# Scores and mask of a head in one 128-row contraction, and a first pair handled in two halves

## The chip, the cores and the metric

The kernel runs on one core of a Trainium2 chip. The metric is the device time of one execution in microseconds; lower is better. The core has five engines with an instruction queue each: TensorE (PE; its weight loads are shown as PEld), VectorE (DVE), ScalarE (ACT), GpSimd (POOL) and SyncE (SP), which mostly issues DMA transfers. Every engine works its queue strictly in order and waits on semaphores for the others.

## The reference

Attention over selected chunks, followed by a gated linear unit with a causal convolution. Batch 4, 8 heads, 768 tokens, head size 64, chunks of 32 tokens, float32 in and out.

```python
k_min, k_max = min and max of k over each chunk of 32 tokens
ub = np.sum(np.maximum(q[:, :, :, None, :] * k_min[:, :, None, :, :],
                       q[:, :, :, None, :] * k_max[:, :, None, :, :]), axis=-1)
ub = np.where(pos[:, None] // chunk >= np.arange(nc)[None, :], ub, -1e9)
top_chunks = np.argsort(ub, axis=-1)[..., -6:]
mask = (chunk of key j is in top_chunks) & (pos[:, None] >= pos[None, :])
attn = softmax(where(mask, q @ k.T / sqrt(64), -1e9));  attn_out = attn @ v

x = attn_out with its heads side by side                       # (4, 768, 512)
gate = sigmoid(sum_k conv_w[k] * xp[:, k:k+S, :])              # 5 taps, causal
out = (gate * (x @ w_val)) @ w_out
```

Query tokens below 192 have at most six chunks to choose from, so no chunk is masked for them.

## The kernel before

**Pairs.** Two heads are handled together as a pair; there are 16, four to a batch. The head size is 64, so the two heads of a pair fill the 128 partitions: head 0 in rows 0 to 63, head 1 in rows 64 to 127 (`HP`).

**Stages of a pair.** K and Q are loaded token by token and turned by TensorE (`tr`, line 472). ScalarE evicts K to the 16-bit `Kh` (`kev`, 478) and Q, times 64, to `Qh` (`qev`, 514). VectorE takes minimum and maximum of every chunk of K from PSUM (`kred`, 484), GpSimd makes the small factors `KB` from them (`ksmall`, 504 to 509). For the bound, Q is split into a 16-bit high part and a rest (`ql`, 522 or 537) and into their positive parts `rh` and `rl` (556, 560, 565). TensorE multiplies these with `KB` (`ub`, 590; for the first four pairs `ubd`, 605). VectorE finds the top six by an eight-largest instruction (`top`, 615 or 644) and writes 1 for each chunk that is not selected to `NS` (`cmp`, 653).

**Mask.** `NS` has the query tokens on partitions and has to be turned to have chunks there. Pairs 0 to 8 do this on TensorE (`selT`, 663) with a copy to `MT` (`mcopy`, 675 on ScalarE for pairs 0 to 2, 677 on VectorE for 3 to 8). Pairs 9 to 15 (`SELD`) do it with a transposing DMA from SyncE's queue (`mdma`, 665).

**Scores.** Scores of a head are computed with the keys on partitions, in six PSUM groups (`BANKS`) of 512, 512, 512, 512, 384 and 256 query columns. A head contracts over 64 rows, so two heads run side by side on the two halves of the array (line 692). For columns from token 192 on, a second matmul per head adds a penalty (line 697): `E` holds -51200 where a key belongs to a chunk, contracted over 64 rows with `MT`. ScalarE takes the exp to `P` (706), GpSimd clears the diagonal blocks (`tri`, 714).

**After the scores.** TensorE multiplies `P` with V and a column of ones (`av`, 735), VectorE divides (743, 744), the result is turned by TensorE (760, 762) or, for pairs 8 to 14, by DMA (`xd`, 765). It goes out to DRAM (`xw`, 778) and back in another layout (`xs`, 782, tile `XS`) for the convolution, which uses 64x32 pieces of the array (793). Then come tanh (799), the value product per batch (816), the gate (824), the output product (840), its eviction (850, 847) and the store (855).

**The order.** Nothing is ordered at run time. Each operation is entered into a graph with an engine, an assumed duration, what it reads and writes, and a key: `p * PERIOD + OFF[stage] + DELTA[stage][p]`. A list scheduler in the program works through the graph and gives each engine the ready operation with the smallest key; it also hands out the eight PSUM banks. The result is one fixed list per engine. `MODE_SWITCH` is the scheduler's price for a change between whole-array and divided-array matmuls. `lock` marks VectorE operations during which it starts no GpSimd work. In the first 26 us, `fill` puts dummy matmuls into TensorE's planned gaps.

Of the kernel before, what the change touches and what calls it, by code (L numbers as in the profile page):

```python
# [11 lines left out]
FP = mybir.dt.float32  # L12
# [7 lines left out]
CH = 32  # L20
# [16 lines left out]
SELD = range(9, NPAIR)  # L37
HP = (slice(0, 64), slice(64, 128))
MP = (slice(0, NCH), slice(64, 64 + NCH))
SM = 192  # L40
# [10 lines left out]
SCORE = [0.40, 0.435, 0.442, 0.445, 0.35, 0.325]  # L51
# [3 lines left out]
for _bi, _segs in enumerate(BANKS):  # L55
    for _col, _jt, _q0, _n in _segs:
        for _i in range(_n // 128):
# [3 lines left out]
            MT=2, on=2, xT=8, XS=3, g=8, gv=8, osb=4, scr=4)  # L61

PERIOD = 13.2487
OFF = dict(wdg=689.463, wbig=-821.57, cw=-638.386, load=-26.611, ktr=-313.189, qtr=-239.905, kev=166.913,
           qev=-383.955, ksm=148.208, spl=244.528, vc=540.922, ub=-278.308, top=-291.823, selT=-172.354,
           sc=-256.234, ex=-198.66, av=-117.315, nrm=263.685, tox=-134.594, xs=14.333, conv=-269.157,
           tanh=-393.525, val=323.303, gv=522.471, out=327.173, ev=91.258)
# [3 lines left out]

EARLY = (0, 1, 2)
QLA = (1, 2, 3)
# [5 lines left out]
    wdg=(-0.259, 11.176, 5.417, 0.077, -1.668, 4.13, 5.35, 1.029, 15.805, 3.045, -3.731, 0, -3.953, 0, 0, 0),  # L79
    wbig=(4.521, -1.173, -4.251, -0.71, -6.836, -7.879, -1.406, -13.108, -0.554, -12.202, 1.098, -1.574,  # L80
        -2.473, -1.919, 10.286, 15.067),
    cw=(0, 0, 1.049, 0, -3.776, -0.311, -0.92, -4.993, -0.92, -6.529, -7.915, -11.168, 0.948, 0, -8.06, 3.706),
    load=(-9.433, -20.842, -32.131, -6.001, -15.044, -1.827, -12.02, 13.514, 5.014, 13.589, 14.754, 5.081,
        -6.414, 4.609, -2.48, -7.659),
    ktr=(-2.8, -5.035, -2.262, 2.581, 0.902, 9.564, 0, 0, 10.923, 1.13, -0.491, -0.903, 0, 13.091, 0, -1.519),
    qtr=(0, -0.071, 9.102, 0, 3.757, 12.574, 5.717, -4.881, -3.114, -14.91, -6.366, 2.222, 0.471, 9.573, 4.53,
        0),
    kev=(-2.229, -2.16, 2.677, -4.88, -7.568, -10.347, 4.307, -2.668, 4.622, 3.276, -0.858, 6.192, 2.689,
        -4.962, -5.387, -2.214),
    qev=(-4.798, -6.316, 0, 0.959, 0, -3.801, -4.226, -3.069, -0.528, -1.223, 0, 0, -6.763, 0, 2.363, 0.065),  # L90
    ksm=(13.028, 3.364, 1.499, 0.759, -1.548, -11.855, -3.051, 6.295, -16.352, 0.972, -0.612, 7.732, 0, -1.146,
        0, -2.064),
    spl=(1.262, 11.137, -16.05, -1.69, -4.33, -6.699, -40.483, 4.206, 3.281, 19.318, -19.036, -16.32, 12.261,
        -5.656, 10.037, 0.718),
    vc=(1.748, -27.085, -4.307, 0, -5.756, -0.371, -4.158, 0.266, 21.35, -3.576, 0, 0.35, 5.25, -0.034, 12.327,
        7.302),
    ub=(-1.261, -1.704, -7.813, 3.091, -4.015, -14.948, 0, 2.233, 2.322, 0, -7.876, 13.15, -8.595, -0.126,
        -18.872, -17.052),
    top=(5.067, 2.169, 6.094, 9.602, 14.045, 13.01, -0.156, -5.897, 1.098, 0.084, 2.913, 2.943, 2.121, -0.002,
        0, 11.724),  # L100
    selT=(10.026, 2.182, -0.498, 4.774, -0.189, -0.821, 5.123, 1.014, 0.873, 3.056, 12.093, 5.215, 1.134,
        -0.467, -2.246, 0.26),
    sc=(-3.684, 2.323, 6.111, 6.751, -2.871, -17.678, -30.23, -1.526, -13.134, -1.219, 1.476, -1.084, 0.465,
        26.912, 1.856, -0.962),
    ex=(0.518, -1.916, 26.612, -0.555, 1.908, 0, -0.304, 1.658, -12.071, 1.68, 0, -4.112, -1.281, 0, -6.681,
        3.816),
    av=(8.141, 23.715, 0, -3.234, 0.925, 0.036, -16.039, -1.518, -0.512, -1.918, -1.793, -11.122, 7.414, 0,
        4.536, 0.431),
    nrm=(0.219, -0.69, -2.27, -15.358, -3.955, -5.17, 1.725, 5.097, 2.136, 76.904, 10.773, 11.399, 0.327,
        10.314, 6.848, 16.568),  # L110
    tox=(5.083, -9.624, -3.531, 16.222, -3.29, 7.771, 0.127, 7.218, -3.237, 2.083, -3.821, -1.177, 0.557,
        -9.325, 3.562, 1.286),
    xs=(-0.589, -20.407, -3.618, 3.816, 0, -1.25, 2.952, -7.384, 2.493, 1.773, 2.46, -0.962, -12.556, 1.62,
        -0.613, 2.66),
    conv=(-0.411, -7.384, -5.199, -0.916, -1.613, -3.484, 2.127, -5.739, 0, 0, 3.767, 12.228, 5.66, -7.854,
        6.314, 3.519),
    tanh=(-0.597, 0.252, -0.042, 6.877, 0, 0, 20.177, 16.64, 2.504, 0.308, 20.302, -0.547, 4.277, 0.743, 5.404,
        6.23),
    val=(0.746, 0, 0, -4.309, -5.054, 0.632, 3.993, -168.145, 0, 0, 4.124, 1.076, -6.197, -6.958, -8.508,
        -6.597),  # L120
    gv=(5.505, -3.972, 0, 7.879, 16.599, -0.597, 3.312, -14.616, -0.18, 0, 4.163, 0.738, 0.401, -3.09, -5.366,
        4.144),
    out=(-0.646, 3.026, -0.113, -7.77, -3.659, 3.789, 4.916, -4.962, 2.461, 0, -1.067, 11.205, -13.796, -2.374,
        -0.072, 0.251),
    ev=(9.081, -6.619, 0.125, -22.323, 0, 0, -4.231, -5.332, 22.655, 3.336, 2.632, -2.286, -26.622, -11.207,
        4.364, 10.267),
# [8 lines left out]
class Graph:  # L135


    def __init__(self, nbuf):
        self.nbuf, self.ops = nbuf, []
        self.reads, self.writes, self.wars, self.after = {}, {}, [], []  # L140

    def op(self, name, eng, occ, key, emit, r=(), w=(), war=(), ps=(), lat=None, mode=None, after=(), dma=None, tail=None,
           lock=False):
        o = Op()
        o.dma, o.tail, o.lock = dma, DMA_TAIL if tail is None else tail, lock
# [15 lines left out]
    def link(self):  # L161
# [3 lines left out]
        def back(x):  # L165
            n = self.nbuf.get(x[0])
            if n is None or len(x) < 2:
                return ()
            y = (x[0], x[1] - n) + x[2:]
            return self.reads.get(y, []) + self.writes.get(y, [])  # L170
# [118 lines left out]
MODE_SWITCH = 0.04  # L289
# [23 lines left out]
def graph(off, period, nbuf):  # L313
# [3 lines left out]
    def key(stage, p, x=0.0):  # L317
        return p * period + off[stage] + off.get((stage, p), 0.0) + x
# [29 lines left out]
    def c_hm():  # L348
        for hh in range(2):
            t.nc.vector.memset(t.hm[HP[hh], hh, :], QS)  # L350
            t.nc.vector.memset(t.hm[HP[hh], 1 - hh, :], 0.0)
# [28 lines left out]
    def c_e():  # L380
        t.nc.scalar.activation(out=t.E.rearrange("p (c t) -> p c t", t=CH),
                               in_=t.id32[:, 0:NCH].unsqueeze(2).to_broadcast([128, NCH, CH]), func=AF.Copy, scale=PEN)
    G.op("E", "ACT", 0.75, -100, c_e, r=[("id32",)], w=[("E",)])
# [31 lines left out]
    last.append(G.op("wout", "POOL", 2.0, key("wbig", 4), w_out, w=[("wout",)], dma=3.2))  # L415
# [4 lines left out]
    cwr = G.op("cwrep", "DVE", 0.7, key("cw", 0), w_rep, r=[("cw",)], w=[("cw4",)])  # L420
# [27 lines left out]
    for p in range(NPAIR):  # L448
# [14 lines left out]
        for x, name in enumerate(("kn", "qn", "vn")):  # L463
            G.op(f"{name}{p}", "SP", 0.6 if x == 2 else 1.1, key("load", p, x + (3 if x == 2 else 0)), load(name), w=[(name, p)], dma=2.0)
# [408 lines left out]
    for o in later:  # L873
        o.deps.add(byname["ksm1"])
# [156 lines left out]
```

## Time and profile before

| | us |
|---|---|
| median of three runs | 188.27 (188.14 to 188.57) |
| the profiled execution, whole | 191.16 |
| its span in the trace | 189.5 |
| first score matmul / last one starts | 14.87 / 155.55 |
| first exp starts | 16.46 |

In the trace, a row of the timeline gives start, length, engine, line, operation, output and inputs, shape and count. A matmul's length runs from its start to a modelled end, and matmuls overlap; what one costs is read from the distance between starts. Groups that the prediction does not show:

```profile
L706 ACT ACTIVATE P<-b 128x512 f16<-128x512 f32 (+2 forms) x192 | 88.8, 593 | 6.2 <-PE b L697 2.1
L484 DVE TENSOR_REDUCE km<-b 128x12 f32<-128x384 f32 x64 | 32.5, 549 | 6.1 <-PE b L472 3.6
L478 ACT ACTIVATE Kh<-b 128x384 f16<-128x384 f32 x32 | 15.9, 529 | 3.7 <-PE b L472 2.9
L514 ACT ACTIVATE Qh<-b 128x384 f16<-128x384 f32 x32 | 15.2, 508 | 3.4 <-PE b L472 3.3
...
XS<-scr SPq DMA_DIRECT2D x32, 194.0 KB, 4.2
...
MT<-NS SPq DMA_TRANSPOSE x7, 4.2
xT<-on SPq DMA_TRANSPOSE x7, 4.9
```

The first four rows are groups of instructions: line, engine, operation, shapes and count, then their busy time in us and the mean of one in ns, then the engine's idle time just before them and what ended it. The last three are DMA issues with the median time from issue to landing. ScalarE's instructions overlap their neighbours by some 0.15 us, so twelve exps of 5376 columns take 5.34 us in the timeline where their means add up to more.

### The profile page before, as it was taken

How to read it: one execution, taken by the hardware profiler on the slowest of the kernel's cores; microseconds unless marked ns; L12 is line 12 of the kernel's file. 1: busy time of each engine (PE TensorE's matmuls, PEld its weight loads, DVE VectorE, ACT ScalarE, POOL GpSimd, SP SyncE). 2: the span in 40 equal slices, each digit the busy share in tenths (PEclk: the TensorE clock that was granted, in tenths of full speed). 3: DMA queues.
4: the chain of work that ended last, by engine and by line, in shares of the span. 5: the costliest groups of instructions: out<-in, count | busy, mean ns of one | idle time of the engine just before them, and what ended most of it. 6: DMA issues, size and time to landing. Idle time of an engine off the chain costs nothing.

```text
span 189.5 us, 7611 instructions
## 1 busy us (share of the span) xinstructions
PE 177.9 (94%) x2994; PEld 118.3 (62%) x2994; DVE 138.0 (73%) x452; ACT 145.3 (77%) x326; POOL 88.1 (46%) x187
## 2 busy tenths in 40 slices
PE   7879999999999999999999999999999897799992
PEld 2566768777677658667766765767666554444540
DVE  4696998699989987999996889897964321621551
ACT  4659999989979788799949998969999496056221
POOL 5336899997981851716154563538464021000000
PEclk9999999999999999999999999999999999999999
DMA  6999979998899988877999999999969969967335
GB/s 143 220 218 210 212 172 196 225 214 195 218 232 263 219 201 205 192 179 211 168 221 215 218 201 205 179 221 196 193 173 196 251 194 194 321 219 244 121 120 212
DMA packets 97105, 38.77 MB, mean 205 GB/s; under 512 B 86810, under 2 KB 91950, under 8 KB 97070
## 3 DMA queue, kind: packets, MB, share of 16 engines
q1 hardware_dynamic: 95966, 37.25, 91.0%
q0 software_dynamic: 1104, 1.05, 3.8%
q8 instruction: 23, 0.38, 0.9%
q14 instruction: 12, 0.10, 0.1%
HBM read 27.34 MB, written 9.47 MB: 194 GB/s over the span
## 4 chain that ended last, share of the span: by engine, by line
PE 68%; DMA 9%; ACT 7%; DVE 5%; POOL 5%; issue 2%; SPq 2%; ACTq 0%; DVEq 0%; POOLq 0%
PE b L735 10%; PE b L692 9%; PE b L840 9%; PE b L816 9%; PE b L472 9%; PE b L793 8%; DMA XS<-scr 7%; PE b L697 6%; PE b L590 5%; ACT P L706 4%; DMA qn<-in_q_dram 2%; DVE km L484 1%; PE b L663 1%; ACT Qh L514 1%; PE b L760 1%
## 5 line engine op out<-in xcount | busy, mean ns | idle before, releaser
L706 ACT ACTIVATE P<-b 128x512 f16<-128x512 f32 (+2 forms) x192 | 88.8, 593 | 6.2 <-PE b L697 2.1
L714 POOL TENSOR_SCALAR_AFFINE_SELECT P<-P 128x512 f16<-128x512 f16 (+1 forms) x64 | 33.9, 551 | 44.9 <-ACT P L706 44.8
L692 PE MATMUL b<-Qh,Kh 64*128 64x128 f16 (+3 forms) x384 | 39.8, 259 | 0.6 <-ACT P L706 0.6
L484 DVE TENSOR_REDUCE km<-b 128x12 f32<-128x384 f32 x64 | 32.5, 549 | 6.1 <-PE b L472 3.6
L697 PE MATMUL b<-MT,E 64*128 64x128 f16 (+4 forms) x352 | 36.9, 255 | 0.1
L824 DVE SCALAR_TENSOR_TENSOR gv<-g,b 128x384 f16<-128x384 f32 x32 | 17.1, 549 | 15.6 <-PE b L816 13.9
L735 PE MATMUL b<-VA,P 128*128 128x65 f16 x672 | 27.7, 194 | 0.0
L735 PEld LDWEIGHTS <-P 128*128 128x128 f16 x672 | 24.4, 98 | 4.3 <-issue 2.3
L692 PEld LDWEIGHTS <-Kh 64*128 64x128 f16 x384 | 17.6, 94 | 12.8 <-issue 8.0
L799 ACT ACTIVATE g<-b 128x384 f32<-128x384 f32 x32 | 14.1, 497 | 14.4 <-PE b L793 14.3
L816 PE MATMUL b<-xT,wval 128*128 128x384 f16 x128 | 24.5, 327 | 0.0
L840 PE MATMUL b<-wout,gv 128*128 128x512 f16 x96 | 23.0, 379 | 0.0
L850 ACT ACTIVATE osb<-b 128x512 f32<-128x512 f32 x21 | 12.9, 637 | 10.6 <-PE b L840 6.7
L697 PEld LDWEIGHTS <-E 64*128 64x128 f16 x352 | 17.3, 94 | 4.7 <-issue 2.0
L793 PE MATMUL b<-XS,WD 64*32 64x384 f16 x640 | 16.5, 324 | 3.3 <-DMA XS<-scr 3.3
L478 ACT ACTIVATE Kh<-b 128x384 f16<-128x384 f32 x32 | 15.9, 529 | 3.7 <-PE b L472 2.9
L744 DVE TENSOR_TENSOR on<-b,rcp 128x384 f16<-128x384 f32 x32 | 17.8, 558 | 1.1
L514 ACT ACTIVATE Qh<-b 128x384 f16<-128x384 f32 x32 | 15.2, 508 | 3.4 <-PE b L472 3.3
L816 PEld LDWEIGHTS <-wval 128*128 128x128 f16 x128 | 11.4, 98 | 9.9 <-issue 3.0
L560 DVE SCALAR_TENSOR_TENSOR rl<-Qh,ql 128x640 f16<-128x640 f16 x16 | 14.6, 911 | 2.2 <-ACT ql L537 2.2
L472 PE MATMUL b<-ident,qn 128*128 128x128 f32 x96 | 14.7, 281 | 0.5 <-ACT P L706 0.3
L472 PE MATMUL b<-ident,kn 128*128 128x128 f32 x96 | 14.4, 283 | 0.5 <-DMA kn<-in_k_dram 0.3
(87 smaller groups left out, 288.2 us busy)
## 6 DMA issues: line engine op xcount, KB each, us to landing
XS<-scr SPq DMA_DIRECT2D x32, 194.0 KB, 4.2
kn<-in_k_dram SPq DMA_DIRECT2D x32, 192.0 KB, 4.8
qn<-in_q_dram SPq DMA_DIRECT2D x32, 192.0 KB, 4.5
vn<-in_v_dram SPq DMA_DIRECT2D x16, 384.0 KB, 5.4
out_dram<-osb SPq DMA_DIRECT2D x24, 256.0 KB, 3.6
scr<-xT SPq DMA_DIRECT2D x32, 97.0 KB, 4.0
wvn<-in_moe_w_val_dram POOLq DMA_DIRECT2D x1, 512.0 KB, 6.8
wout<-in_moe_w_out_dram POOLq DMA_DIRECT2D x4, 128.0 KB, 6.4
```

Source lines behind the costliest of these rows:

```text
L472: t.nc.tensor.matmul(out=b[:, j * 128:(j + 1) * 128], lhsT=vv(name, p)[:, 3 * w + j, :], rhs=t.ident, is_transpose=True, start=(j == 0), s ...
L484: t.nc.vector.tensor_reduce(out=vv("km", p)[:, i, w * 12:(w + 1) * 12], in_=bank(("kn", p, w))[:, 0:HB].rearrange("p (c t) -> p c t", t=CH ...
L692: nc.tensor.matmul(out=bb[hh][:, col:col + n], lhsT=kh[HP[hh], jt * 128:(jt + 1) * 128], rhs=qh[HP[hh], q0:q0 + n], start=(si == 0), stop= ...
L697: nc.tensor.matmul(out=bb[hh][:, col + m0 - q0:col + n], lhsT=t.E[HP[hh], jt * 128:(jt + 1) * 128], rhs=mt[HP[hh], m0 - 128:q0 + n - 128], ...
L706: t.nc.scalar.activation(out=t.P[p % 2][hh][bi], in_=bank(("s", p, bi, hh))[:, 0:n], func=AF.Exp, scale=0.125 / QS)
L714: t.nc.gpsimd.affine_select(out=ap, in_=ap, pattern=[[0, n], [1, 128]], compare_op=ALU.is_ge, fill=0.0, base=0, channel_multiplier=-1)
L735: t.nc.tensor.matmul(out=b[:, qt, :], lhsT=t.P[p % 2][hh][bi][:, col:col + 128], rhs=vv("VA", p)[:, hh, jt, :], start=(jt == 0), stop=(jt ...
L744: t.nc.vector.tensor_tensor(out=vv("on", p)[:, :, hh * 64:(hh + 1) * 64], in0=b[:, :, 0:D], in1=rc.unsqueeze(2).to_broadcast([128, NT, D]) ...
L793: t.nc.tensor.matmul(out=bank(("cv", p, r))[32 * g:32 * g + 32, 0:HB], lhsT=t.WD[HP[r], g * 20 + k * 4 + p % 4, :], rhs=x[HP[r], g * XH + ...
L816: t.nc.tensor.matmul(out=k[:, 0:HB], lhsT=t.wval[:, ct, et * 128:(et + 1) * 128], rhs=t.xT[:, (4 * b_ + ct) % 8, XL + w * HB:XL + (w + 1) ...
L824: t.nc.vector.scalar_tensor_tensor(out=vv("gv", 4 * b_ + et)[:, sl], in0=vv("g", 4 * b_ + et)[:, sl], scalar=1.0, in1=bank(("val", b_, et, ...
L840: t.nc.tensor.matmul(out=k, lhsT=vv("gv", 4 * b_ + et)[:, s * 128:(s + 1) * 128], rhs=t.wout[:, et, :], start=(et == 0), stop=(et == NCT - 1))
```

## The change

**Scores.** `Kh` and `Qh` get a second plane and become 128 x 2 x 768. Plane `hh` of `Kh` holds head `hh`'s keys in that head's 64 rows, and the penalty `E` in the other 64. Plane `hh` of `Qh` holds that head's queries in its rows, and its transposed `NS` in the other 64 (zeros for tokens 0 to 127). One matmul over 128 rows then gives scores plus penalty; there are 24 per pair, one head after the other. `MT` and the separate `E` tile are gone. `hm` exchanges its halves, so that each head's bound lands with the columns that belong in the other head's rows.

**What feeds it.** `E` is written once into each of the three `Kh` buffers (two fills on ScalarE, three on VectorE, one on GpSimd). K is evicted once per head and half, by 64-row instructions. Q is evicted without its first 128 columns, these follow per head by 64-row instructions of 128 columns, and VectorE copies head 1's remaining 640 columns to plane 1 (`qcp`). The mask is copied per head from the PSUM transpose into `Qh` by VectorE, except head 1 of pairs 1 and 2 and a part of pair 0, on ScalarE. `SELD` is empty: all pairs turn `NS` on TensorE.

**First pair.** For pair 0 (`HALF`) the loads of K and Q, the minima and maxima, `KB`, `rl`, the bound, top six, compare, transpose and mask copy are divided in two by tokens; K is loaded from SyncE's queue and Q from ScalarE's, and the small operations for `KB` move from GpSimd to VectorE. `QLA` takes in pair 0, whose rest of Q is then made by TensorE and ScalarE. Pair 0's operations up to the mask have keys before everything else.

**Order.** Some assumed durations change, and `PERIOD`, `OFF` and `DELTA` are all replaced.

```diff
-SELD = range(9, NPAIR)
+SELD = ()
-MP = (slice(0, NCH), slice(64, 64 + NCH))
-SM = 192
-SCORE = [0.40, 0.435, 0.442, 0.445, 0.35, 0.325]
+SCORE = [0.44, 0.435, 0.435, 0.435, 0.33, 0.23]
-PERIOD = 13.2487
+PERIOD = 13.7715
...
+FIRST = dict(ktr=0, qtr=1, kev=1, ksm=2, qev=2.5, spl=3, ub=4, top=5, selT=6)
+HALF = (0,)
+MCX = (1,2)
-QLA = (1, 2, 3)
+QLA = (0,1,2,3)
...
-MODE_SWITCH = 0.04
+MODE_SWITCH = 0.125
...
     def key(stage, p, x=0.0):
+        if p in HALF and stage in FIRST:
+            return FIRST[stage] - 260 + x
         return p * period + off[stage] + off.get((stage, p), 0.0) + x
...
+    def c_e(i, hh):
+        def emit():
+            sl = HP[1 - hh]
+            out = t.tiles["Kh"][i][sl, hh, :].rearrange("p (c t) -> p c t", t=CH)
+            src = t.id32[sl, 0:NCH].unsqueeze(2).to_broadcast([64, NCH, CH])
+            if i == 0:
+                t.nc.scalar.activation(out=out, in_=src, func=AF.Copy, scale=PEN)
+            else:
+                (t.nc.vector if i + hh < 3 else t.nc.gpsimd).tensor_scalar(out=out, in0=src, scalar1=PEN, scalar2=None, op0=ALU.mult)
+        return emit
...
+        def loadh(name, w, p=p, b_=b_, h0=h0):
+            def emit():
+                e = t.nc.sync if name == "kn" else t.nc.scalar
+                for hh in range(2):
+                    e.dma_start(out=vv(name, p)[:, 3 * w:3 * w + 3, hh * 64:(hh + 1) * 64],
+                                in_=getattr(t, name[0])[b_, h0 + hh].rearrange("(t p) d -> p t d", p=128)[:, 3 * w:3 * w + 3])
+            return emit
...
-        def kev(w, p=p):
-            def emit():
-                t.nc.scalar.activation(out=vv("Kh", p)[:, w * HB:(w + 1) * HB], in_=bank(("kn", p, w))[:, 0:HB],
+        def kev(w, hh, p=p):
+            def emit():
+                t.nc.scalar.activation(out=vv("Kh", p)[HP[hh], hh, w * HB:(w + 1) * HB], in_=bank(("kn", p, w))[HP[hh], 0:HB],
                                        func=AF.Copy)
             return emit
...
+        def qe0(hh, p=p):
+            def emit():
+                t.nc.scalar.activation(out=vv("Qh", p)[HP[hh], hh, 0:128], in_=bank(("qn", p, 0))[HP[hh], 0:128],
+                                       func=AF.Copy, scale=QS)
+            return emit
...
+        def qcp(p=p):
+            (t.nc.gpsimd if p in QCP else t.nc.vector).tensor_copy(out=vv("Qh", p)[HP[1], 1, 128:S], in_=vv("Qh", p)[HP[1], 0, 128:S])
...
+        def mcopy(hh, p=p):
+            def emit():
+                src = t.MT[p % 2] if p in SELD else h16(("sel", p))
+                (t.nc.scalar.copy if p in MCA or p in MCX and hh else t.nc.vector.tensor_copy)(
+                    out=vv("Qh", p)[HP[1 - hh], hh, 128:S], in_=src[HP[1 - hh], 0:NIT * 128])
+            return emit
...
         def score(bi, p=p):
             def emit():
-                nc, kh, qh, mt = t.nc, vv("Kh", p), vv("Qh", p), vv("MT", p)
-                bb = [bank(("s", p, bi, hh)) for hh in range(2)]
+                kh, qh = vv("Kh", p), vv("Qh", p)
                 segs = BANKS[bi]
-                for si, (col, jt, q0, n) in enumerate(segs):
-                    last = si == len(segs) - 1
-                    m0 = max(q0, SM)
-                    masked = m0 < q0 + n
-                    for hh in range(2):
-                        nc.tensor.matmul(out=bb[hh][:, col:col + n], lhsT=kh[HP[hh], jt * 128:(jt + 1) * 128],
-                                         rhs=qh[HP[hh], q0:q0 + n], start=(si == 0), stop=(last and not masked),
-                                         skip_group_check=True)
-                    if masked:
-                        for hh in range(2):
-                            nc.tensor.matmul(out=bb[hh][:, col + m0 - q0:col + n],
-                                             lhsT=t.E[HP[hh], jt * 128:(jt + 1) * 128],
-                                             rhs=mt[HP[hh], m0 - 128:q0 + n - 128], start=False, stop=last,
-                                             skip_group_check=True)
+                for hh in range(2):
+                    b = bank(("s", p, bi, hh))
+                    for si, (col, jt, q0, n) in enumerate(segs):
+                        t.nc.tensor.matmul(out=b[:, col:col + n], lhsT=kh[:, hh, jt * 128:(jt + 1) * 128], rhs=qh[:, hh, q0:q0 + n],
+                                           start=(si == 0), stop=(si == len(segs) - 1), skip_group_check=True)
             return emit
```

## The prediction

> **What bounds the kernel now.** I read the page's busy line first, then the waits of TensorE, then TensorE's timeline around the scores, then the windows. The lines, in that order:
>
> ```profile
> PE 177.9 (94%) x2994; PEld 118.3 (62%) x2994; DVE 138.0 (73%) x452; ACT 145.3 (77%) x326; POOL 88.1 (46%) x187
> PEclk9999999999999999999999999999999999999999
> PE b L793 <- DMA XS<-scr: 3.3, 3, 1.3
> PE b L345 <- DVE warm L339: 1.3, 1, 1.3
> PE b L663 <- DVE NS L653: 0.6, 1, 0.6
> ...
> 100.76 0.20 PE L590 MATMUL b<-KB,ql 128*128 128x80 f16 x1
> 100.89 0.39 PE L692 MATMUL b<-Qh,Kh 64*128 64x512 f16 x2
> 101.12 0.38 PE L697 MATMUL b<-MT,E 64*128 64x512 f16 x2
> 101.33 0.27 PE L692 MATMUL b<-Qh,Kh 64*128 64x256 f16 x2
> 101.44 0.27 PE L697 MATMUL b<-MT,E 64*128 64x256 f16 x2
> 101.55 0.22 PE L692 MATMUL b<-Qh,Kh 64*128 64x128 f16 x2
> 101.61 0.22 PE L697 MATMUL b<-MT,E 64*128 64x128 f16 x2
> 101.76 0.22 PE L590 MATMUL b<-KB,rh 128*128 128x96 f16 x1
> ...
> 14.90:40.00 25.10, 24.19 (x448) 18.50 (x448) 20.49 (x71) 24.74 (x59) 22.50 (x42) 1.00 1.06 202
> 100.00:130.00 30.00, 30.00 (x503) 20.04 (x500) 24.96 (x82) 27.01 (x62) 15.46 (x32) 1.00 1.07 210
> 156.60:189.50 32.90, 26.63 (x345) 13.71 (x342) 11.31 (x22) 11.59 (x25) 0.77 (x2) 1.00 0.68 203
> ```
>
> TensorE hardly waits for anybody (three waits on the XS transfer, little else) at full clock, and its timeline has no gaps in the middle: it is the bound from the first score (14.87) to the last (155.55). In the windows ScalarE (fifth column) is nearly full in the first stage too, 24.74 of 25.10, and 27.01 of 30.00 later. At the end, 156.6 to 189.5, TensorE works 26.63 of 32.90 us.
>
> The timeline shows what a burst of half-array scores costs. Inside it, a two-head pair of 512 columns starts 0.21 after the one before, a pair of 128 columns 0.055: two heads side by side cost what one would. At its edges, the 80-column matmul at 100.76 (0.04 elsewhere) holds the next start off for 0.13, and the last pair, worth 0.055, holds it off for 0.15. So each edge costs about 0.10 us. I counted 54 such bursts in the timeline: 108 edges, 10.8 us.
>
> **What the Trainium skill says.** "TensorEngine Tiling (Array Packing)", Key Properties: changing the tiling mode drains TensorE, and tiles run independently; the 0.10 at each edge and the 0.055 per pair agree. "ScalarE: Activation LUTs", What ACT_TABLE_LOAD costs: one element per cycle and lane at 1.2 GHz, back-to-back instructions overlapping; so half the partitions save nothing. The trace agrees on the first part (twelve exps of 512, 384 and 256 columns in 5.34 us, about 0.05 + n/1200 each); no half-partition activation is in it. "VectorE: DVE Perf Modes", the perf-mode tier table: a 16-bit copy from SBUF runs at up to 4x, from PSUM at up to 2x; L677, 640 columns from PSUM, took 0.49 with its latency, which fits 2x.
>
> **The change part by part.** Counts are from the order in which the changed program's instructions stand on each engine; durations are spacings in the trace of before.
>
> *TensorE.* Before, a pair streams 2688 columns of scores and 2432 of mask, heads side by side: 5120/2400 = 2.13, in the timeline 2.21 (the stretch 140.24 to 141.90 is 1.66 for 3840 columns, 1.6 at 2.4 per ns). After, 24 matmuls over 128 rows, 2 x 2688 columns, 2.24 plus a few ns each: 2.31. That adds 0.1 x 16 = 1.6 us. The switches go: 10.9, as only the convolution's 24 stay (133 before, all kinds). Seven pairs (9 to 15) get their mask by five TensorE transposes instead of a DMA: 7 x 0.3 = +2.1. The first pair's quarter more: +0.4. Net -6.8 us.
>
> *ScalarE.* K is evicted per head: 64 instructions of 384 columns for 32, +32 x 0.37 = +11.8. Q's first eviction shrinks from 384 to 256 columns, 16 x -0.11 = -1.7, and 32 pieces of 128 columns come, 0.16 each (by the slope of the others, below half of a 384): +5.1. The rest (second E row set, one more ql, smaller mask copies) about +0.9. Sum +16. Cover: ScalarE was idle for some 24 us between its first exp (16.46) and its last (157.9), while TensorE set the pace. If that cover were gone, the whole 16 would show. From the changed order, 132.5 us of ScalarE work stand between the two exps, 117.0 before.
>
> *VectorE.* 16 copies of Q's second head (4x, 0.23) +3.7; mask copies 28 of 640 columns and a few shorter for 6 before, 0.40 each, +9.5; three E fills of 0.87. About +15 on 138.0: 81% of a similar span, hidden unless its stages meet the others'.
>
> *SyncE and DMA.* Seven mask transposes leave the queue (1.2 to 2.3 us of issue each, 4.2 to landing) and with them a wait of the queue on NS. The head of the queue loads pair 0's K in halves, ScalarE's queue loads its Q: four issues of 0.5 us before its table load (1.28) and two E fills (0.69 each), so its first eviction is at about 5.6, against 5.33 before.
>
> *First pair.* The chain of before, from Q's landing to the first mask copy:
>
> ```profile
> 2.48 3.84 DMA qn<-in_q_dram
> 7.01 0.49 ACT Qh L514
> 9.17 1.03 DVE rl L560
> 10.20 1.86 DVE km L484 x4
> 12.06 0.83 DVE top L615 x10
> 12.99 0.42 DVE NS L653
> 13.46 0.45 PE b L663 x5
> ```
>
> The 1.86 is pair 1's. In the changed order pair 1's four reductions still stand among pair 0's on VectorE, the E fills ahead of them, and GpSimd's small operations (7.70 to 9.52) move to VectorE in two sets of five. In order from 5.8: reductions 0.93, small set 0.6 to 1.2, Q copy 0.23, rl 0.33, reductions 0.93, rl 0.47, small set again, max 0.36, reductions and compares 2.26, max 0.54, two copies 0.77: 13.8 to 15.0. So halves bring the first score to 14.4, 0.5 earlier, no more. But all scores of pair 0 then go in one run, so its first exp is at 14.9 for 16.46.
>
> *Stages.* I add the work of each engine between the first score (first exp) of one pair and the next, at the spacings of the trace: on TensorE 0.113 for a K or Q transpose (six in 0.68), 0.033 for an AV matmul (42 in 1.41), 0.94 for a convolution of 40, 0.163 and 0.217 for L816 and L840, 0.03 to 0.045 for a bound matmul of L590, 0.0575 for a 16-bit transpose, scores as above; on ScalarE 0.05 + n/1200; on VectorE 0.066 + n/960 (four reductions of 384 in 1.95), copies over 2 or 4. Pairs 0 to 2: ScalarE 12.5 + 8.1 + 5.1 = 25.7, TensorE only 19.6 (ScalarE evicts K and Q of pairs 2 and 3 between the exps). Before, the same stretch took 14.87 to 36.8 = 21.9. So ScalarE binds there and costs 3.8. Pairs 3 to 14: TensorE 105.6 (before 110.7), ScalarE 101.3. Before took 114.15 (36.8 to 150.95), 3.45 above its sum; so 109.05, and 1.5 (0 to 4) for two engines at 92 to 96% in lockstep: 110.55. From pair 15's first score to the end: 38.5 before. TensorE's sum falls by 0.5; of 2.5 us of XS waits there I take 1.5 off, since the queue is freed of mask transposes, and 10.3 us of matmuls now stand between the last output transpose and the last convolution, whose way (copy 0.5, issue and landing 4.9, then 5.3) is about 10.7: 36.5.
> Sum: 14.4 + 25.7 + 110.55 + 36.5 = 187.15, against 189.5. The profiled execution took 191.16 in all, 1.66 around its span, and was 2.9 above the median; scaled by 188.27/189.5 the forecast is 186.0.
>
> **Rivals.**
> *TensorE's whole saving arrives* (ScalarE keeps up early): 189.5 - 5.6 - 0.5 - 1.5 = 181.9, scaled 180.7. For it: TensorE is the bound. Against: ScalarE's 25.7 us in one stretch cannot be packed.
> *Nothing is left*: the last convolutions hang on XS transfers (4.3 to 5.2 us each) whatever TensorE saves, and ScalarE's loss eats the rest: 188.3. For it: the three XS waits.
> *Slower, by three full engines.* In pairs 3 to 14 the order is fixed, ScalarE has 92% and VectorE about 85% of TensorE's time, and a mask now goes compare, transpose, copy on VectorE before its scores. If every stage ended with its slowest engine, the sum of maxima for the three is 122, 13 above TensorE alone (overstated: VectorE's work is due at other times). From 3.9 us of such stalls on (the 1.5 taken and 2.4 more) it is slower; at 6.5 the span is 192.2, scaled 190.9. Against: in 14.9 to 40 ScalarE at 98.6% and TensorE at 96% ran side by side.
>
> **How the numbers follow.** Forecast 0.50, whole saving 0.10, nothing left 0.12, slower 0.28. About 0.2% is what a measurement of this kernel can tell from no change. Faster 0.60, same 0.12, slower 0.28. The range leaves out most of the whole-saving case and the end of the slow one: 182.0 to 190.8. The unknown costs lie inside: coupling 0 to 4; the first score 13.8 to 15.2; a 128-column eviction 0.16, between 0.11 (elements alone) and 0.26 (the 256-column one), -1.6 to +3.2 over 32; a 128-row score matmul between 0.053 per 128 columns and the 0.06 of a mask transpose, -0.3 to +2. The likeliest case's own range is 184.3 to 187.9.
>
> **What would show it.** Right: no half-array matmul left but the convolution's; scores of one pair at 2.3 us of TensorE; first exp near 15, pair 3's near 40 with ScalarE full until then; ScalarE 160 us busy or more, TensorE about 171 with a few more waits on ScalarE. Wrong: TensorE waiting on VectorE's mask copies in mid-kernel, half-partition evictions much off 0.37, the first score at 12 or 17, or longer XS waits at the end.

## The result, and the profile after

| | before | after |
|---|---|---|
| median, us | 188.2 (187.24 to 188.57, 4 runs) | 200.07 (199.19 to 200.96, 4 runs) |
| ratio to before | 1 | 1.0639, 95% interval 1.0575 to 1.0704 |
| span of the profiled execution, us | 189.5 | 197.5 |

The changed kernel is 6.4% slower, where 1.2% faster was forecast. Before's profiled execution was a long one, 191.16 us against a median of 188.2, so before's stages below add up to some 3 us more than in its usual run. The page of the changed kernel's profiled execution, its busy line, its clock line and its chain line (the shares of the span in the chain of work that ended last; "issue" is time in which an engine waited for nothing that the profile shows), and then before's chain line:

```profile
PE 176.7 (89%) x2675; PEld 125.1 (63%) x2675; DVE 159.7 (81%) x505; ACT 166.9 (84%) x394; POOL 90.8 (46%) x189
PEclk9969999999999999999999999999999999999998
PE 46%; DVE 25%; ACT 22%; issue 5%; ACTq 0%; DVEq 0%
```

```profile
PE 68%; DMA 9%; ACT 7%; DVE 5%; POOL 5%; issue 2%; SPq 2%; ACTq 0%; DVEq 0%; POOLq 0%
```

The groups of the new and changed work (busy us, mean ns of one | idle before):

```profile
L853 PE MATMUL b<-Qh,Kh 128*128 128x128 f16 (+3 forms) x384 | 49.9, 258 | 4.3 <-DVE mub L769 1.3
L527 ACT ACTIVATE Kh<-b 64x384 f16<-64x384 f32 x64 | 31.2, 489 | 2.5 <-DVE km L546 1.8
L827 DVE COPY Qh<-b 64x640 f16<-64x640 f16 x28 | 13.6, 485 | 2.1 <-PE b L819 1.8
```

The windows of the stages that the forecast used (first score of pair 0, of pair 3, of pair 15, end); the columns are length, busy us of PE, PEld, DVE, ACT and POOL with instruction counts, granted clock, DMA share and GB/s. First before, then after:

```profile
14.90:36.60 21.70, 21.09 (x400) 16.04 (x400) 18.37 (x66) 21.69 (x52) 19.43 (x36) 1.00 1.03 196
36.60:151.00 114.40, 112.45 (x2053) 77.63 (x2048) 96.44 (x326) 97.99 (x223) 60.82 (x125) 1.00 1.02 208
```

```profile
16.20:45.00 28.80, 23.19 (x352) 17.74 (x351) 23.93 (x78) 27.35 (x66) 20.86 (x40) 1.00 1.01 183
45.00:161.40 116.40, 110.29 (x1821) 82.67 (x1820) 108.42 (x352) 110.60 (x267) 57.90 (x120) 1.00 0.85 195
161.40:197.50 36.10, 31.91 (x425) 17.69 (x421) 14.10 (x28) 16.95 (x37) 2.81 (x6) 0.97 0.61 180
```

Read the PE and ACT columns. Before, TensorE worked 133.5 of the 136.1 us of these first two stages and set the pace. After, the stages last 145.2 us and TensorE stands idle for 11.7 of them (its busy time, 133.5 again, contains the modelled tail of a matmul at each gap; e9 below, with the same matmuls, counts 129.4). ScalarE works 138.0 of the 145.2 (95%), VectorE 132.4 (91%). TensorE no longer sets the pace alone: ScalarE is now the fullest engine in these stages, with VectorE close behind, and their shares of the chain rise from 7% and 5% to 22% and 25%.

Stage by stage, from the first score matmuls of the pairs (e9 is an experiment below):

| stage, us | before | forecast | after | e9 |
|---|---|---|---|---|
| to the first score | 14.9 | 14.4 | 16.2 | 16.1 |
| pairs 0 to 2 | 21.7 | 25.7 | 28.8 | 25.7 |
| pairs 3 to 14 | 114.4 | 110.55 | 116.4 | 109.4 |
| pair 15 to the end | 38.5 | 36.5 | 36.1 | 36.2 |
| span | 189.5 | 187.15 | 197.5 | 187.4 |

So the span is missed by 10.35 us: 1.8 + 3.1 + 5.85 - 0.4. TensorE's own part came as forecast. Its timeline in mid-kernel:

```profile
99.52 1.89 PE L994 MATMUL b<-wout,gv 128*128 128x512 f16 x8
101.25 0.93 PE L853 MATMUL b<-Qh,Kh 128*128 128x512 f16 x6
102.05 0.49 PE L914 MATMUL b<-identh,on 128*128 128x128 f16 x6
```

From 99.52 to 101.25 there are 1.73 us for eight output matmuls of 512 columns, 0.216 each: nothing is paid between them and the scores. Before, such an edge cost 0.093 (median over the trace).

What takes the time is in ScalarE's timeline. Start, length, instruction:

```profile
22.63 0.55 ACT L527 ACTIVATE Kh<-b 64x384 f16<-64x384 f32 x1
23.00 0.55 ACT L597 ACTIVATE Qh<-b 128x384 f16<-128x384 f32 x1
...
24.34 0.49 ACT L667 ACTIVATE rh<-b 128x384 f16<-128x384 f32 x1
24.73 0.47 ACT L527 ACTIVATE Kh<-b 64x384 f16<-64x384 f32 x1
25.10 0.26 ACT L603 ACTIVATE Qh<-b 64x128 f16<-64x128 f32 x1
25.37 0.49 ACT L527 ACTIVATE Kh<-b 64x384 f16<-64x384 f32 x1
25.89 0.49 ACT L636 ACTIVATE ql<-b 128x384 f16<-128x384 f32 x1
26.40 0.27 ACT L603 ACTIVATE Qh<-b 64x128 f16<-64x128 f32 x1
26.70 2.00 ACT L527 ACTIVATE Kh<-b 64x384 f16<-64x384 f32 x4
28.71 0.39 ACT L597 ACTIVATE Qh<-b 128x256 f16<-128x256 f32 x1
```

The eviction at 22.63 writes head 0's rows, which start at partition 0, and the next instruction, of 128 rows, also starts at partition 0: it begins 0.37 later, while the first still runs (0.55). The four at 26.70 go from head to head, 0, 64, 0, 64: they take 2.00 us, 0.50 each, and none begins before its predecessor ends. I call the first partition that an instruction reads and writes its start partition; in these kernels it is 0 or 64. Wherever two neighbours in an engine's queue have different ones (a change of start), the spacing is longer. Sorted by that, the medians over the whole trace:

| spacing from start to start, us | same start partition | start partition changes |
|---|---|---|
| ScalarE, 384 columns | 0.371 (64 rows and 128 rows) | 0.496 (0 to 64), 0.510 (64 to 0) |
| ScalarE, 128 columns | 0.157 (at 0), 0.177 (at 64) | 0.281, 0.297 |
| ScalarE, exp of 512 columns | 0.478 | 0.615 (one case) |
| VectorE, mask copy of 640 columns | 0.398 | 0.487, 0.525 |
| VectorE, reduction of 384 columns | 0.465 | 0.578 |

In program order the start partition changes 93 times on ScalarE and 70 times on VectorE, before 0 and 2 times. At some 0.125 and 0.11 each that is up to 11.6 and 7.7 us of engine time (an estimate from the table: where the second of two neighbours has to wait for its data anyway, nothing is lost). "ScalarE: Activation LUTs" of the Trainium skill, What ACT_TABLE_LOAD costs, says that ACTIVATEs back to back overlap by about 93 ns; here it is about 120 ns (a 384-column eviction lasts 0.49 us and its successor starts after 0.371), and it is there only between neighbours with the same start partition.

### The profile page after: what moved, and what is told of

Its sections match the earlier page's. It is cut to its first block, busy times and chain, and to the rows that moved or that the text cites. A ratio compares the mean times of both kernels' runs of the same rounds, so it can differ in the third digit from the quotient of the medians.

```text
span 197.5 us, 7062 instructions
## 1 busy us (share of the span) xinstructions
PE 176.7 (89%) x2675; PEld 125.1 (63%) x2675; DVE 159.7 (81%) x505; ACT 166.9 (84%) x394; POOL 90.8 (46%) x189
## 4 chain that ended last, share of the span: by engine, by line
PE 46%; DVE 25%; ACT 22%; issue 5%; ACTq 0%; DVEq 0%
PE b L853 10%; PE b L970 9%; ACT P L860 9%; PE b L994 8%; ACT Kh L527 7%; DVE km L546 5%; PE b L947 5%; PE b L889 4%; PE b L521 4%; DVE on L898 3%; DVE Qh L827 3%; PE b L703 2%; DVE ql L621 2%; ACT Qh L597 2%; PE b L364 2%
## 5 line engine op out<-in xcount | busy, mean ns | idle before, releaser
L860 ACT ACTIVATE P<-b 128x512 f16<-128x512 f32 (+1 forms) x192 | 88.2, 594 | 2.0 <-PE b L853 1.5
L868 POOL TENSOR_SCALAR_AFFINE_SELECT P<-P 128x512 f16<-128x512 f16 (+1 forms) x64 | 36.2, 585 | 54.4 <-ACT P L860 53.4
L853 PE MATMUL b<-Qh,Kh 128*128 128x128 f16 (+3 forms) x384 | 49.9, 258 | 4.3 <-DVE mub L769 1.3
L853 PEld LDWEIGHTS <-Kh 128*128 128x128 f16 x384 | 28.8, 97 | 17.0 <-issue 8.0
L527 ACT ACTIVATE Kh<-b 64x384 f16<-64x384 f32 x64 | 31.2, 489 | 2.5 <-DVE km L546 1.8
L889 PEld LDWEIGHTS <-P 128*128 128x128 f16 x672 | 25.4, 98 | 3.9 <-POOL P L868 1.6
L970 PEld LDWEIGHTS <-wval 128*128 128x128 f16 x128 | 11.8, 97 | 8.6 <-issue 1.6
L690 POOL CAST VA<-vn 128x768 f16<-128x768 f32 x16 | 13.2, 827 | 5.0 <-DMA vn<-in_v_dram 3.8
L521 PE MATMUL b<-ident,kn 128*128 128x128 f32 x96 | 14.9, 280 | 0.6 <-ACT Kh L527 0.4
L827 DVE COPY Qh<-b 64x640 f16<-64x640 f16 x28 | 13.6, 485 | 2.1 <-PE b L819 1.8
L994 PEld LDWEIGHTS <-gv 128*128 128x128 f16 x96 | 8.8, 97 | 9.9 <-issue 0.8
L597 ACT ACTIVATE Qh<-b 128x256 f16<-128x256 f32 (+1 forms) x32 | 13.7, 458 | 1.3 <-PE b L521 1.1
```

Of the source, the lines that this page charges most:

```text
L521: t.nc.tensor.matmul(out=b[:, j * 128:(j + 1) * 128], lhsT=vv(name, p)[:, 3 * w + j, :], rhs=t.ident, is_transpose=True, start=(j == 0), s ...
L527: t.nc.scalar.activation(out=vv("Kh", p)[HP[hh], hh, w * HB:(w + 1) * HB], in_=bank(("kn", p, w))[HP[hh], 0:HB], func=AF.Copy)
L827: (t.nc.scalar.copy if p in MCA or p in MCX and hh else t.nc.vector.tensor_copy)(out=vv("Qh", p)[HP[1 - hh], hh, 128:S], in_=src[HP[1 - hh ...
L853: t.nc.tensor.matmul(out=b[:, col:col + n], lhsT=kh[:, hh, jt * 128:(jt + 1) * 128], rhs=qh[:, hh, q0:q0 + n], start=(si == 0), stop=(si = ...
L860: t.nc.scalar.activation(out=t.P[p % 2][hh][bi], in_=bank(("s", p, bi, hh))[:, 0:n], func=AF.Exp, scale=0.125 / QS)
L868: t.nc.gpsimd.affine_select(out=ap, in_=ap, pattern=[[0, n], [1, 128]], compare_op=ALU.is_ge, fill=0.0, base=0, channel_multiplier=-1)
```

## The experiments

Every kernel was timed against the kernel before on the same chip; before's medians there were 189 to 190 us, so ratios are compared. In the short diffs the lines with a minus are the changed kernel's (those of e11 and e12 the kernel before's). A, B and C are the theories that the expectations name.

**e1: ScalarE's half evictions made whole.** K per head and Q's first 128 columns are written with 128 rows from partition 0; same order. The rows of the penalty get the other head's keys instead.

```diff
-out=vv("Kh", p)[HP[hh], hh, w * HB:(w + 1) * HB], in_=bank(("kn", p, w))[HP[hh], 0:HB]
+out=vv("Kh", p)[:, hh, w * HB:(w + 1) * HB], in_=bank(("kn", p, w))[:, 0:HB]
```

> ScalarE's half evictions of K and Q write all 128 rows from partition 0 instead of 64 rows of one half; columns, number and order of all instructions stay (the penalty rows of K's planes are overwritten, so the scores are not the reference's). Theory A, start partition: two neighbours on ScalarE overlap only where both start at the same partition, else the second waits for the first's end, 0.13 us; the changed kernel has 93 such changes on ScalarE, here 3, so 11 us of ScalarE's time go, and ScalarE is the bound from 16 to 162: 189 to 193 us. Theory B, too many ScalarE instructions (64 evictions for 32 at 0.37 each): nothing changes, 199 to 201. Theory C, VectorE and its mask copies set the pace: 197 to 200.

Measured: 195.19 us, ratio 1.0289 (1.0233 to 1.0344), from 1.0639. More than half of the loss goes, which neither B nor C allows, but the time stays above A's range. ScalarE is left with 3 changes of start, VectorE keeps its 70. More rows, less time.

**e2: the same on VectorE**, for Q's copy and the mask copies (these now carry the other head's rows along, in e3 and e7 too).

```diff
-out=vv("Qh", p)[HP[1 - hh], hh, 128:S], in_=src[HP[1 - hh], 0:NIT * 128])
+out=vv("Qh", p)[:, hh, 128:S], in_=src[:, 0:NIT * 128])
```

> Only VectorE's half copies (Q's second head, the masks) are widened to 128 rows from partition 0, ScalarE's stay; number and order stay (planes get rows of the other head, so the scores are not the reference's). Theory A: 64 of 70 changes of the start partition on VectorE go, 0.11 us each, 7 us of its time, but ScalarE stays the bound with 91 changes: 197 to 199.5. Theory B: 199 to 201. Theory C: 191 to 195.

Measured: 201.16 us, ratio 1.0599 (1.0521 to 1.0677): no gain to be seen, and above A's range. Two accidents that the trace shows lie on top: VectorE's `rl` (see e3), and a TensorE clock at 0.50 from 25.8 to 32.6 us.

**e3: e1 and e2 together.**

> Both of the former together: 1 change of the start partition left on ScalarE and 6 on VectorE, same instructions in the same order (scores not the reference's). Theory A: what was forecast without it, 186 to 189 us, with first score about 0.5 us earlier. Theory B: 198 to 201. Theory C: as with VectorE's alone, 191 to 195.

Measured: 194.92 us, ratio 1.0269 (1.021 to 1.0329), hardly below e1 and far above the 186 to 189 that A gave. The trace shows what came in between: from pair 3 to pair 4 e3 takes 13.4 us where the changed kernel takes 9.2. In that stretch TensorE waits once for 3.7 us on VectorE's `rl`, and after the wait its clock stands at 0.50 for 3.4 us. e3's VectorE, e3's GpSimd, and then the same `rl` in the changed kernel:

```profile
42.25 5.07 DVE L662 SCALAR_TENSOR_TENSOR rl<-Qh,ql 128x640 f16<-128x640 f16 x1
```

```profile
42.34 2.39 POOL L444 COPY wval<-wvn 128x512 f16<-128x512 f16 x4
44.69 3.12 POOL L868 TENSOR_SCALAR_AFFINE_SELECT P<-P 128x512 f16<-128x512 f16 x5
```

```profile
45.38 0.93 DVE L662 SCALAR_TENSOR_TENSOR rl<-Qh,ql 128x640 f16<-128x640 f16 x1
```

`rl` reads two SBUF tensors. In e3 it starts as GpSimd goes into an unbroken run of nine copies and clears, and ends during the ninth. e2 has the same accident (`rl` takes 3.71 us, and pair 3 to 4 takes 12.4). So I compare pair 4 to pair 15, which it doesn't touch: after 107.2 us, e2 105.7, e1 103.3, e3 101.3 (before 105.1). ScalarE's part is 3.8, VectorE's 1.5, both together 5.9.

**e4: fewer evictions.** Head 1's 32 K evictions are left out (its rows are filled with zeros once).

```diff
         def kev(w, hh, p=p):
             def emit():
+                if hh:
+                    return
```

> The second head's 32 K evictions are left out (its plane holds zeros instead of keys, so its scores lack the keys); planned order otherwise kept. On ScalarE 32 instructions of 0.50 us and 58 of 93 changes of the start partition go, about 16 + 3 us. Theory A and B both say that ScalarE is no longer the bound: A 187 to 191, B 184 to 189 (then 16 us of work, not the start partition, is what was too much). Theory C: 195 or more.

Measured: 192.88 us, ratio 1.0152 (1.0094 to 1.0209), above the ranges of A and B, with the `rl` accident in it too (4.60 us). It shows that ScalarE's eviction work is on the path, but not whether its number or its price is at fault, as the evictions take their changes of start with them.

**e5: no halves in the first pair.**

```diff
-HALF = (0,)
+HALF = ()
```

> The first pair is not halved (loads, bound, compare and mask copy of pair 0 in one piece, its small operations on GpSimd again, its keys from the table, which was not tuned for that); everything else of the change stays. If the halves brought the 0.5 us that was forecast, the first score comes at 16.5 to 18 and the end 0 to 2 us later: 199 to 202 us. If the two sets of five small operations on VectorE (measured about 0.24 us each) cost what the halves gain, 198 to 200. If the halves are what made the changed kernel slow, 195 or less.

Measured: 211.61 us, ratio 1.1202 (1.1134 to 1.1269). No expectation covers that. The first score comes at 18.7 instead of 16.2, but pairs 0 to 2 take 32.1 and the end 43.6 as well: the keys were found for the halves, and the whole order comes out different. What the halves gain or cost can't be read from this run.

**e6 and e7: the accident removed.** GpSimd's four weight copies (line 444) are moved behind a clear of pair 3; e6 is the changed kernel with that alone, e7 is e3 with it.

```diff
     order = fill(G, order, t)
+    later = [o for o in order if o.name.startswith("wperm")]
+    order = [o for o in order if o not in later]
+    at = [o.name for o in order].index("tri3.01") + 1
+    order[at:at] = later
```

> Control: the changed kernel with GpSimd's four weight permutations moved behind two of its mask operations of pair 3, away from VectorE's operation for rl of pair 4. In the changed kernel these did not collide, so all theories say the same: 198 to 201 us.

> All half-partition instructions of ScalarE and VectorE widened to 128 rows from partition 0 (scores not the reference's), and the weight permutations moved as in the control, because in the first such run VectorE's rl (two inputs from SBUF) of pair 4 took 5.07 us while GpSimd worked through these. Theory A with this accident as the rest: span 189 to 190, so 190.5 to 191.5 us, ratio to before 1.00 to 1.01, pair 3 to 15 in 110 to 112 us as forecast. If another cost holds the kernel, it stays at 194 to 196 us.

Measured: e6 200.13 us, ratio 1.056 (1.0506 to 1.0613), as expected, so the move alone brings little or nothing; e7 190.74 us, ratio 1.0071 (1.0041 to 1.0101), in A's range. Same number of instructions, same columns, same order: e7 takes 9.4 us less than e6, by rows and start alone.

**e9: rows and start told apart.** Until here every instruction that lost its change of start also went from 64 to 128 rows. e9 keeps 64 rows but puts all of them at rows 0 to 63, in e6's order with six small fills of GpSimd added. It computes without the penalty and without head 1's part.

```diff
-out=vv("Kh", p)[HP[hh], hh, w * HB:(w + 1) * HB], in_=bank(("kn", p, w))[HP[hh], 0:HB]
+out=vv("Kh", p)[HP[0], hh, w * HB:(w + 1) * HB], in_=bank(("kn", p, w))[HP[0], 0:HB]
...
-out=vv("Qh", p)[HP[1 - hh], hh, 128:S], in_=src[HP[1 - hh], 0:NIT * 128])
+out=vv("Qh", p)[HP[0], hh, 128:S], in_=src[HP[0], 0:NIT * 128])
...
-PEN = -100.0 * 8.0 * QS
+PEN = 0.0
```

> Every half-partition instruction of ScalarE and VectorE (K per head, Q's first 128 columns per head, Q's copy, the mask copies) keeps its 64 rows, its columns and its place in the order, but all of them read and write rows 0 to 63; GpSimd's weight copies stand where e6 has them, and six small fills of GpSimd in its idle time cover the rows that nothing writes. It leaves out head 1's part of the products and the penalty (its factor is zero). Theory A, the start partition (a change of it costs the overlap of two neighbours, about 0.13 on ScalarE and 0.11 on VectorE, whatever the number of rows): as e7, 190.7 us, 189.7 to 191.7; a 384-column K eviction in a run then costs 0.37 from start to start. Rival B, the number of rows (an instruction of 64 rows costs more than one of 128): as e6, 199 to 200, and 0.50 per eviction stays.

Measured: 189.12 us (188.89 to 189.43), ratio 1.0003 (0.9982 to 1.0024), 0.6 us below A's range and 10 below B's. Why it is also below e7 stays open. ScalarE has 1 change of start left, VectorE 6. ScalarE's timeline in e9, the same instructions as in the changed kernel's above:

```profile
22.51 0.55 ACT L533 ACTIVATE Kh<-b 64x384 f16<-64x384 f32 x1
22.89 0.55 ACT L603 ACTIVATE Qh<-b 128x384 f16<-128x384 f32 x1
...
24.26 0.58 ACT L533 ACTIVATE Kh<-b 64x384 f16<-64x384 f32 x1
24.63 0.37 ACT L609 ACTIVATE Qh<-b 64x128 f16<-64x128 f32 x1
24.79 0.59 ACT L533 ACTIVATE Kh<-b 64x384 f16<-64x384 f32 x1
25.16 0.59 ACT L642 ACTIVATE ql<-b 128x384 f16<-128x384 f32 x1
25.53 0.39 ACT L609 ACTIVATE Qh<-b 64x128 f16<-64x128 f32 x1
26.07 1.61 ACT L533 ACTIVATE Kh<-b 64x384 f16<-64x384 f32 x4 [0.16 <-PE b L527]
27.57 0.38 ACT L603 ACTIVATE Qh<-b 128x256 f16<-128x256 f32 x1
```

The four evictions now take 1.50 us to the next start, 0.375 each, and the 128-column piece at 24.63 costs 0.16; over all 64 evictions the median is 0.371, over the 28 mask copies of VectorE 0.398. An instruction's own length is not shorter (0.58 at 24.26, where the same one in the changed kernel, at 24.73, has 0.47); only the next one begins earlier. e9's windows:

```profile
16.10:41.80 25.70, 22.55 (x351) 17.54 (x350) 22.91 (x78) 24.99 (x65) 24.22 (x43) 1.00 1.12 202
41.80:151.20 109.40, 106.80 (x1819) 81.91 (x1818) 104.15 (x352) 104.97 (x267) 57.96 (x121) 1.00 0.89 208
```

For the same work ScalarE is busy 130.0 us in these stages against 138.0 in the changed kernel, VectorE 127.1 against 132.4, and the stages are 10.1 us shorter. TensorE's clock is at 1.00 in these stages in both kernels, so the zeros in e9's data did not help by the clock. The number of rows is ruled out as the cause, and the change of start is what is left.

**e10: the whole computation with fewer changes.** The bound's Q lies in plane 1, VectorE copies head 0's half down to plane 0 (which spares two of its four changes per pair), and the order is found anew with the changes priced.

```diff
+ROW = dict(ACT=0.13, DVE=0.11)
...
+                        if o.row != row[e]:
+                            occ += ROW[e]
+                        row[e] = o.row
```

> The changed kernel's whole computation, with the start partition in the order's prices (0.13 ScalarE, 0.11 VectorE per change) and the order found anew for it; the bound's Q lies in plane 1 and VectorE copies head 0's half down to plane 0, so that two of its four changes per pair go. ScalarE's changes fall from 93 to 83, VectorE's from 70 to 38: 1.3 and 3.5 us of work. Theory A: 191 to 194, since the order no longer lets VectorE and ScalarE arrive late by 10 us; it stays above before, as ScalarE keeps 10 us of lost overlap. Rival (the order is good and only the 9 us of lost overlap matter, of which a third goes here): 196 to 198.

Measured: 193.16 us (192.77 to 194.02), ratio 1.0208 (1.0128 to 1.0288), as expected. Two thirds of the loss can be had back without giving up the change, but it stays slower than before. In the trace the gain is in pairs 3 to 14 (111.9 us for 116.4), and pairs 0 to 2 still take 28.9. ScalarE's 83 remaining changes of start are the likely reason; that they are was not tested.

**e11 and e12: the other lesson applied to the kernel before.** If edges between whole and half arrays cost 0.093 us each, an order that has fewer of them should help the kernel before as it is. e11 finds the whole order anew with that price, e12 only what comes after pair 3.

```diff
-MODE_SWITCH = 0.04
+MODE_SWITCH = 0.093
```

> The kernel before with all its instructions, only in another order: the order is found anew with 0.093 us as the price of a change between whole-array and divided-array matmuls (0.04 before), which leaves 117 such changes for 133. If the edges that TensorE pays are what the kernel before can still save: 16 x 0.093 = 1.5 us less, 186 to 187.5 beside 188 to 189.5 for before, ratio about 0.99. If the stalls of an order that was not made for these engines eat it: 188 to 191.

> The kernel before with all its instructions; its order is kept as it is up to pair 3 and found anew after that, with 0.093 us as the price of a change between whole-array and divided-array matmuls: 122 changes are left of 133, so 11 x 0.093 = 1.0 us less of TensorE's work, and up to as much again by a tail that is packed closer. If e11 lost its time in the first three pairs alone (7.0 us later there, 2.7 and 2.9 us earlier in the two stages after): ratio 0.985 to 0.995 of before. If a new order is as such worse on the chip than the one that before has: 1.00 to 1.02.

Measured: e11 195.23 us, ratio 1.0327 (1.022 to 1.0435), a miss of both expectations. Pairs 0 to 2 take 28.7 us there instead of 21.7. Windows of 2 us in that stretch:

```profile
20.00:22.00 2.00, 1.73 (x29) 0.85 (x23) 2.00 (x2) 2.00 (x6) 2.00 (x2) 1.00 0.87 172
22.00:24.00 2.00, 0.82 (x12) 0.79 (x12) 2.00 (x14) 1.54 (x4) 1.52 (x3) 0.74 1.10 248
24.00:26.00 2.00, 2.00 (x44) 1.79 (x41) 1.58 (x8) 0.66 (x2) 0.88 (x2) 0.50 1.32 235
26.00:28.00 2.00, 2.00 (x19) 1.97 (x17) 1.09 (x11) 0.69 (x1) 2.00 (x4) 0.50 1.32 223
```

The new order put the filter's preparation early: VectorE's two copies of the filter took 1.74 us (beside three casts of GpSimd), TensorE stood still for 1.3 us until they were done, and in that pause its granted clock (third column from the end) fell to 0.50. The trace has it there from 22.95 to 29.78, 6.8 us, which is worth up to 3.4 us of TensorE's work, half of the 7 us that the stretch is longer. e12, which keeps the first pairs' order, ran at 189.6 us, ratio 0.996 (0.993 to 0.9991): 0.4% faster than before, just outside the 0.985 to 0.995 that was expected, and by its ratio the fastest of all kernels here. In its trace 2.2 us are waited for an XS transfer near the end (at 152.4), and after that TensorE's clock stands at 0.50 for 3.4 us. That keeping the first pairs' order takes away e11's loss fits the reading above.

## Why the prediction was wrong

**TensorE: right in its parts.** The forecast had the edges gone (108 at about 0.10; measured 0.09 to 0.10 before, and after only the convolution's 24) and a pair's scores at 2.31 us; they take 2.30 (16 matmuls of 0.056, two of 0.109, two of 0.162, four of 0.216). The sum, -6.8 us, can't be read exactly, since busy time contains tails: 177.9 us before and 173.0 in e9 make -4.9. That TensorE was the bound before was right as well.

**ScalarE: the step that failed.** The forecast priced "64 instructions of 384 columns for 32, +32 x 0.37 = +11.8" and "32 pieces of 128 columns come, 0.16 each". The reasoning "so half the partitions save nothing" is true and was taken for a price; it only says that the instruction isn't cheaper. In the order in which they stand, the evictions cost 0.50 and the pieces 0.28, because a neighbour with another start partition can't overlap. With 93 changes that is up to 11.6 us more on an engine that the forecast had at 92% of TensorE's time; e9, without them, is 10.1 us shorter in the first two stages. The forecast itself had named "half-partition evictions much off 0.37" as a sign of being wrong. The trace of before had no such pair of neighbours on ScalarE, and the forecast said so ("no half-partition activation is in it"), but no range was given for the 384-column one at all, and the 128-column one's upper end, 0.26, was taken from whole-partition rows.

**VectorE: the same error, smaller.** Mask copies at 0.40 measured 0.487 and 0.525 next to a change of start, and 70 changes come to up to 7.7 us. e1 to e3 put its share at 1.5 to 2.0 of 5.9 us between pairs 4 and 15.

**Pairs 0 to 2 and pairs 3 to 14: right, once that price is taken out.** e9 gives 25.7 for a forecast 25.7, and 109.4 for 110.55, with 0.4 us added for two full engines instead of 1.5. e7, which has as few changes of start, gives 26.7 and 110.2, so the exact hit is in part luck. That ScalarE binds in the first stretch held, and it costs 7.1 there where 3.8 was forecast.

**The first score: wrong by 1.8 us, and only in part explained.** It was put at 14.4 (13.8 to 15.2) and came at 16.2, in e9 at 16.1, so start partitions aren't it. The forecast added up VectorE's operations in their order, but left out pair 1's Q copy among them and whatever VectorE and TensorE wait for. One operation, the cast to `KB` at 7.39 us, takes 0.85 us where its repetition takes 0.19. And work of pair 1 stands ahead of pair 0's on two engines:

```profile
14.05 0.75 ACT L805 COPY Qh<-b 64x256 f16<-64x256 f16 x2
15.47 0.50 ACT L667 ACTIVATE rh<-b 128x384 f16<-128x384 f32 x1
16.02 0.32 PE L629 MATMUL b<-Qh,identn 128*128 128x384 f16 x1 [0.73 <-ACT rh L667]
16.18 0.33 PE L853 MATMUL b<-Qh,Kh 128*128 128x128 f16 x3
```

The mask copies that the first three scores need end at 14.80 on ScalarE, but in TensorE's queue a matmul for pair 1's Q stands ahead of them, and it waits 0.73 us for ScalarE's `rh` of pair 1. VectorE too waits 0.87 us for pair 1's Q before it makes pair 0's last mask copies (15.96 to 16.69). TensorE's clock is at 0.50 from 11.3 to 14.7 us as well. e10 keeps the full clock there and still has its first score at 16.0, in another order; what each of these costs was not tested alone.

**The end: right.** 36.1 for a forecast 36.5. Of the 2.5 us that TensorE waited for XS transfers in this stage before, none is left after; the forecast had taken 1.5 off.

**The scaling: wrong, and hidden by the rest.** e9 has the forecast's span almost exactly, 187.4 us for 187.15 (its first score is 1.7 later, its pairs 3 to 14 are 1.15 shorter, so there is luck in it). It takes 189.12 us, that is its span and 1.7, and its ratio to before is 1.0003. The forecast had multiplied its span by 188.27/189.5, before's median over the span of one profiled execution, and so came to 186.0 where adding the 1.7 gives 188.85. Even with the right price for the pieces, 1.2% faster was not to be had.

**The rivals.** "Slower, by three full engines" named the engines that turned out full, but its mechanism was stalls between them and its price at most 6.5 us, which gave 190.9. In e9, with full engines and cheap neighbours, such stalls are almost absent. The changed kernel's whole loss over e9, 10.1 us in the span, comes with the price of the instructions themselves, which no rival had. And even without it the change gains nothing: e9 is at 1.0003 of before. By the stages of the table, the first score (+1.2 us) and pairs 0 to 2 (+4.0, where ScalarE's added evictions stand) take back 5.2 of the 7.3 us that pairs 3 to 14 and the end save; the rest does not show in the medians.

## What to carry to other kernels

Before work is cut into pieces for half the partitions, look at what will stand next to each piece in its engine's queue: on ScalarE and VectorE a piece that starts at another partition than its neighbour (0 and 64 here; others were not tried) loses the overlap, which adds a third to a 384-column eviction on ScalarE and four fifths to a 128-column one. Put pieces with the same start next to each other, or let the pieces be whole. Add up a chain with the work of others that stands between in the queue, and don't scale a span from one profile by the median of other runs. And where a trace shows no instance of an operation, "it isn't cheaper" is one bound only: the upper one needs a reason too, above all on an engine that is near full.

## What the runs showed of the hardware

The start partition (0 or 64): spacings of 0.371 against 0.496 to 0.510 us on ScalarE and 0.398 against 0.487 to 0.525 on VectorE, whatever the number of rows (the table above and e9).

VectorE held by GpSimd: `rl`, with two SBUF inputs, took 5.07 us where it takes 0.93, while GpSimd ran nine instructions without a break. "GPSIMD Engine Reference" of the Trainium skill, Specifications, says that GpSimd's SBUF interfaces are shared with VectorE, with contention for instructions of two SBUF inputs. The trace agrees, and shows that the delay can last over several GpSimd instructions: 4 us, of which 3.7 came through to TensorE. It does not always come: in the changed kernel `rl` took 0.93 us beside an unbroken run that was even longer (43.8 to 50.0). What decides is not shown.

The clock: in a pause of TensorE of 1.3 us (21.9 to 23.2) e11's granted clock fell to 0.50, and it stayed there for 6.8 us. The changed kernel has a stretch of 3.4 us at 0.50 (11.3 to 14.7), with no pause above 0.72 us in the 3.4 us before it. "TensorE: Matmul & The Clock Gate", What's actually happening, has the array at half clock after an idle window of about 3.4 us, and at full clock again after a busy one as long. The halving agrees, and so do the stretches of 3.4 us and of twice that; but the pauses here were much shorter than the page's idle window.
